# Attention with memory slots and two wide layers on one core: turns of a quarter, a quarter and a half for the first two batches

## The chip, the cores and the metric

The kernel runs on one core of a Trainium2 chip. The metric is the device time of one execution in microseconds (us), the median of the runs shown.

## The reference

Four batches of 576 tokens, 8 heads of 64. `phi` weighs the tokens of a head into 32 memory slots: a softmax over tokens, so its maximum and its sum run over 576 tokens. Queries attend to these 32 slots only. Two dense layers follow, 512 to 2048 to 512 each, with weights in float64.

```
a = exp(phi - max(phi, tokens)); a = a / (sum(a, tokens) + 1e-9)
k_m = einsum('bhsm,bhsd->bhmd', a, k); v_m = einsum('bhsm,bhsd->bhmd', a, v)
attn = softmax(q @ k_m^T / 8)                 # over the 32 slots
x = attn @ v_m                                # 2304 tokens x 512
x = leaky_relu(x @ w_in, 0.01) @ w_out        # first layer
out = mish(x @ w2_in) @ w2_out                # second layer
```

## The kernel before

A hand-written planner (class Order) puts all work in order before anything runs. Each piece of work (a task) has a priority in units of items, estimated engine durations, dependencies and buffers that it takes or uses. The planner walks through estimated time, at each moment gives a free engine the ready task of lowest priority, and so fixes the instruction order of every engine and of the DMA queue on SP. A task that takes a buffer may start at most WIN = 8 items ahead of the current item. On the chip each engine then runs its list strictly in order: an instruction whose input is late holds back all that stands behind it. For a load the planner assumes bytes divided by 300e3 per us, after those in front, plus fixed terms (L130, L294).

First layer. An item is one block of 128 hidden channels (m, 16 of them) for one half of a batch (sub, 288 tokens): 6 matmuls of at x vw into h_t (L862; vw is v_m times w_in for a quarter of four m, a chunk), two leaky relus on ACT, one giving hi_t, one e_t (L876), their difference lo_t on DVE (L883), and two items later 12 matmuls of w_out into four accumulators (L895). There are 128 items. At the end of a turn (a run of m for one batch) the accumulators are copied to x1, or added to it by DVE where an earlier turn wrote there (L940). Batches 0 and 1 share a chunk's decoded weights. Before, their turns are (L721): batch 0 chunk 0, batch 1 chunk 0, batch 0 chunk 1, batch 1 chunk 1, batch 0 chunks 2 and 3, batch 1 chunks 2 and 3, so that batch 1 starts at item 8; batches 2 and 3 follow whole, from items 64 and 96.

Preparation of a batch, in two groups g of four heads (kv_tasks, L429): load phi, k, v; the maximum over tokens by folding 6 rows to 3 (L449), then 3 to 1 by two further DVE operations (L451); a transpose on PE (L458), a reduce (L464), a diagonal matrix (L465), a broadcast by a matmul with ones (L471), four subtractions on DVE (L479), Exp on ACT; the same fold for the sum where b > 0, one matmul for the sum (L506); the matmuls for k_m and v_m (L495). score_tasks (L565) loads and transposes q (L582), multiplies, and half (L626) does the softmax over slots; the result is at_t, hi and lo (L298, L314). Group 1 of batches 0 and 1 has buffers of its own in a pool that is later closed (`sp = "s" if b < 2 and g == 1`, L430, L566); its space goes to the w_out blocks 8 to 15.

Weights: load_raw (L330) loads raw 512 KB of float64, decode (L352) makes float32 of it with ACT and DVE (L362, L364, L369, L371, L379, L389), hi_lo (L305) splits it in two parts. w_chunk(c) (L747) decodes four raw blocks of w_in into two win buffers and writes them to DRAM, from where later batches load them; wo_unit(m) (L733) does a block of w_out. Second-layer weights are decoded between the items from priority W2 = 48 on (L814) and written to DRAM. The second layer (units of L1208 and L1274) follows.

Priorities: batch 1's preparation starts A1 = 13 items ahead of its first item, group 1 S1 = 2 later; A2 = 30 and S2 = 10 for batches 2 and 3. Loads of w_out and w_in go WOL = 3 ahead of their decode, which is WO = 2 and WC = 4 ahead of the item. Buffers of a tag are given out in the order in which the code creates them (L795 to L810): chunk 0, batch 1 with its vw of chunk 0, chunk 1, and so on. FILL = 60 small matmuls (L776) occupy PE at the start.

Of the kernel before, what the change touches and what calls it, by code (L numbers as in the profile page):

```python
# [81 lines left out]
class Order:  # L82
# [10 lines left out]
    def run(self, window):  # L93
# [13 lines left out]
        while left:  # L107
            ready.sort(key=lambda t: (t.prio, t.n))
            hit = False
            for t in list(ready):  # L110
# [47 lines left out]
def kernel(  # L158
# [134 lines left out]
    def mb(shape_bytes):  # L293
        return shape_bytes / 300e3  # L294
# [134 lines left out]
    def kv_tasks(b, g, p0, dp):  # L429
        sp = "s" if b < 2 and g == 1 else ""  # L430
# [23 lines left out]
        t0 = keep(add({"DVE": 0.9}, p0, lambda e: fold(rmax, ALU.max), [l_phi], [rmax], [ph]))  # L454
        mt = ps_tag.new([P, PR])
        t1 = add(
            {"PE": 0.1}, p0 + dp,
            lambda e: nc.tensor.transpose(mt.make(), rmax.t[:, 0].rearrange("p h m -> p (h m)"), ident[:PR, :PR]),  # L458
            [t0], [mt], [rmax],
        )  # L460
        mx, dg = tags["mx" + sp].new([P, 1]), tags["dg" + sp].new([P, P])

        def fmax(e):
            nc.vector.tensor_reduce(out=mx.make(), in_=mt.t, axis=AX.X, op=ALU.max)  # L464
            nc.vector.tensor_scalar(out=dg.make(), in0=ident, scalar1=mx.t, scalar2=None, op0=ALU.mult)  # L465
# [916 lines left out]
```

## Time and profile before

| | |
|---|---|
| median of 3 runs | 804.36 us (802.5 to 805.64) |
| the profiled execution, its own time | 806.19 us |
| its span | 804.3 us |
| PE busy | 773.1 us, 96% |
| DVE, ACT busy | 558.4 us, 69%; 394.6 us, 49% |
| granted TensorE clock, mean | 0.982 |

The 20-us slices of the page show the stages: up to 42 us the preparation of batch 0, from 42 to 424 us the 128 items of the first layer with the preparation of batches 1 to 3 and the decoding of weights between them, from 424 us the second layer. A short matmul's record ends by a model, and a busy engine may still be at a low granted clock, so stretches are read with the clock beside them. Engines run their lists in order: an idle time in front of an instruction is put down to what it waited for, which need not be what PE needed.

### The profile page before, as it was taken

The numbers are of one execution on the slowest core, as the hardware profiler recorded it, in microseconds if no ns is written. First come the engines' busy times: TensorE is split into PE (matmuls) and PEld (weight loads), VectorE is DVE, ScalarE is ACT, GpSimd is POOL, SyncE is SP. The second block draws the span as 40 slices with busy tenths as digits, with TensorE's granted clock in tenths as the row PEclk, the third lists the DMA queues.
The fourth block names the chain that finished last, engine by engine and source line by source line (L and its number), as shares of the span: only waits on it lengthen the run. The fifth ranks groups of instructions, "written<-read, shape, count | busy, mean of one in ns | idle before, by whom it ended". The sixth has DMA issues, their size and how long they took to land.

```text
span 804.3 us, 13708 instructions
## 1 busy us (share of the span) xinstructions
PE 773.1 (96%) x5300; PEld 701.9 (87%) x5300; DVE 558.4 (69%) x1198; ACT 394.6 (49%) x857; POOL 0.7 (0%) x6
## 2 busy tenths in 40 slices
PE   7897999999999999999999999999999999999995
PEld 6686998898888998999999889888988998899884
DVE  4898879877876887661666667696666698566432
ACT  2667566745453555543555444454443355444322
POOL 0000000000000000000000000000000000000000
PEclk8899899999998999999999999999999999999998
DMA  9995599656867667400222210023010014000002
GB/s 219 257 275 162 174 266 274 216 168 223 268 218 220 207 199 261 160 27 1 79 79 78 81 53 26 27 80 106 26 51 29 1 53 131 27 27 27 0 1 78
DMA packets 43136, 97.61 MB, mean 121 GB/s; under 512 B 3904, under 2 KB 24384, under 8 KB 43072
## 3 DMA queue, kind: packets, MB, share of 16 engines
q1 hardware_dynamic: 42912, 96.48, 39.0%
q8 instruction: 41, 0.67, 0.3%
q10 hardware_dynamic: 160, 0.26, 0.1%
q14 instruction: 23, 0.19, 0.1%
HBM read 79.43 MB, written 17.30 MB: 120 GB/s over the span
## 4 chain that ended last, share of the span: by engine, by line
PE 73%; DMA 12%; DVE 9%; ACT 2%; issue 2%; SPq 1%; ACTq 0%; DVEq 0%
PE h_t L1208 22%; PE acc_t L1274 17%; PE acc_t L895 16%; PE misc_t L1274 8%; PE h_t L862 8%; DMA raw_t<-in_moe_w_out_dram 4%; DMA raws_t<-in_moe_w_in_dram 3%; DMA raw_t<-in_moe_w_in_dram 2%; DMA kv_t<-in_v_dram 2%; DMA kv_t<-in_k_dram 1%; DVE raw_t L389 1%; PE misc_t L699 1%; DVE lo_t L883 1%; PE misc_t L495 1%; DMA rawm_t<-in_moe_w_out_dram 1%
## 5 line engine op out<-in xcount | busy, mean ns | idle before, releaser
L895 PE MATMUL acc_t<-hi_t,wo_t 128*128 128x288 f32 x1024 | 163.6, 301 | 0.6 <-DVE x_t L300 0.3
L895 PEld LDWEIGHTS acc_t<-hi_t,wo_t 128*128 128x128 f32 x1024 | 144.6, 190 | 8.9 <-issue 4.5
L862 PE MATMUL h_t<-at_t,vw_t 128*128 128x288 f32 x768 | 127.0, 302 | 8.8 <-ACT e_t L876 5.5
L862 PEld LDWEIGHTS h_t<-at_t,vw_t 128*128 128x128 f32 x768 | 111.2, 192 | 11.6 <-ACT e_t L876 7.6
L876 ACT ACTIVATE hi_t<-h_t 128x288 fp32r<-128x288 f32 x128 | 52.9, 413 | 111.2 <-PE acc_t L895 96.9
L883 DVE TENSOR_TENSOR lo_t<-e_t,hi_t 128x288 fp32r<-128x288 f32 x128 | 58.7, 460 | 55.5 <-ACT e_t L876 26.2
L895 PE MATMUL acc_t<-lo_t,wo_t 128*128 128x288 f32 x512 | 91.6, 301 | 1.0 <-DVE lo_t L883 1.0
L1208 PE MATMUL h_t<-xt_t,vw_t 128*128 128x384 f32 x432 | 87.8, 338 | 0.0
L895 PEld LDWEIGHTS acc_t<-lo_t,wo_t 128*128 128x128 f32 x512 | 74.5, 188 | 10.9 <-issue 7.7
L1208 PE MATMUL h_t<-xt_t,wo_t 128*128 128x384 f32 x384 | 82.9, 337 | 0.0
L1208 PEld LDWEIGHTS h_t<-xt_t,vw_t 128*128 128x128 f32 x432 | 77.6, 188 | 6.0
L298 ACT ACTIVATE wo_t<-raw_t 128x512 fp32r<-128x512 f32 (+1 forms) x66 | 36.6, 561 | 86.6 <-PE h_t L1208 84.2
L1274 PE MATMUL acc_t<-wo_t,hi_t 128*128 128x512 f32 x288 | 78.2, 394 | 0.0
L1208 PEld LDWEIGHTS h_t<-xt_t,wo_t 128*128 128x128 f32 x384 | 69.1, 188 | 3.9
L1219 DVE TENSOR_TENSOR x_t<-x_t,h_t 128x384 f32<-128x384 f32 x96 | 52.7, 549 | 19.3 <-PE h_t L1208 19.2
L1274 PEld LDWEIGHTS acc_t<-wo_t,hi_t 128*128 128x128 f32 x288 | 53.6, 188 | 9.7
L298 ACT ACTIVATE vw_t<-raw_t 128x512 fp32r<-128x512 f32 x49 | 30.6, 631 | 58.6 <-PE h_t L1208 58.1
L876 ACT ACTIVATE e_t<-h_t 128x288 f32<-128x288 f32 x128 | 52.5, 410 | 0.1
L362 ACT ACTIVATE raw_t<-raw_t 128x512 f32<-128x512 f32 x43 | 33.2, 773 | 30.3 <-DMA raw_t<-in_moe_w_in_dram 16.9
L1274 PE MATMUL acc_t<-wo_t,lo_t 128*128 128x512 f32 x144 | 45.1, 392 | 0.0
L379 DVE TENSOR_SCALAR raw_t<-raw_t 128x512 uint16<-128x512 uint16 x50 | 37.7, 759 | 8.2 <-ACT raw_t L369 5.7
L1219 DVE TENSOR_TENSOR e_t<-e_t,h_t 128x384 f32<-128x384 f32 x24 | 13.3, 553 | 41.2 <-PE h_t L1208 41.1
(178 smaller groups left out, 1146.4 us busy)
## 6 DMA issues: line engine op xcount, KB each, us to landing
raw_t<-in_moe_w_out_dram SPq DMA_DIRECT2D x24, 512.0 KB, 5.3
win_t<-wscr SPq DMA_DIRECT2D x24, 512.0 KB, 5.2
raw_t<-w2scri SPq DMA_DIRECT2D x24, 512.0 KB, 3.2
raw_t<-in_moe_w_in_dram SPq DMA_DIRECT2D x22, 512.0 KB, 5.3
kv_t<-in_k_dram SPq DMA_DIRECT2D x8, 576.0 KB, 8.0
kv_t<-in_v_dram SPq DMA_DIRECT2D x8, 576.0 KB, 8.9
wscr<-win_t SPq DMA_DIRECT2D x8, 512.0 KB, 7.7
w2scri<-raw_t SPq DMA_DIRECT2D x8, 512.0 KB, 6.4
```

The lines of the kernel that those rows point to most:

```text
L298: nc.scalar.activation(out=o, in_=i, func=AF.Copy)
L362: nc.scalar.activation(out=hf(), in_=hf(), func=AF.Copy, scale=2.0 ** -112)
L379: lambda e: nc.vector.tensor_scalar(out=quarter(1), in0=quarter(3), scalar1=0x8000, scalar2=None, op0=ALU.bitwise_and),
L389: nc.vector.scalar_tensor_tensor(out=out, in0=hw(), scalar=3, in1=lw(), op0=ALU.logical_shift_left, op1=ALU.bitwise_or)
L495: nc.tensor.matmul(out=acc.t[M * h:M * (h + 1), :].rearrange("p (j d) -> p j d", j=2), lhsT=ph.t[:, h, r, :], rhs=kv.t[:, :, h, r, :], sta ...
L862: nc.tensor.matmul(out=h.t, lhsT=us[g][0].t[:, wi, j0:j0 + P], rhs=ats[g][0].t[:, ai, cols], start=(n == 0), stop=(n == 3 * NG - 1),)
L876: nc.scalar.activation(out=o, in_=h.t, func=AF.Prelu, alpha=0.01)
L883: lambda e: nc.vector.tensor_tensor(out=lb.make(), in0=eb.t, in1=hb.t.bitcast(F32), op=ALU.subtract),
L895: nc.tensor.matmul(out=ac[kk].t, lhsT=wu[0].t[:, wi, kk * P:(kk + 1) * P], rhs=(hb if src == 0 else lb).t, start=(first and (wi, src) == ( ...
L1208: nc.tensor.matmul(out=h.t, lhsT=w[:, wi, c0:c0 + P], rhs=xp[b, xi].ap()[:, j], start=(j == 0 and k3 == 0), stop=(j == 1 and k3 == 2),)
L1219: {"DVE": dve(NB2)}, prio, lambda e: nc.vector.tensor_tensor(out=out(), in0=in0(), in1=in1(), op=op), deps, take, use
L1274: nc.tensor.matmul(out=ac[t].t, lhsT=(lb if x else hb).t[:, t * P:(t + 1) * P], rhs=wu[0].t[:, wi, :], start=(first and (wi, x) == (0, 0)) ...
```

## The change

The turns of batches 0 and 1 become a list T: batch 0 chunk 0, batch 0 chunk 1, batch 1 chunks 0 and 1, batch 0 chunks 2 and 3, batch 1 chunks 2 and 3. Batch 1 starts at item 16, chunk 1 is needed at item 8. The code creates chunk and batch tasks in the same order. The folds stop at three rows: PE transposes all three, the reduce goes over 288 columns, three matmuls make the sum. The diagonal may go to ACT. For batch 0 (PB = 1) the subtraction is done by PE: phi times the identity and the diagonal, repeated by its access pattern, times minus one, into the same PSUM tile, in two halves, from which ACT takes Exp; for other batches the four subtractions become one of 768 elements. Only batch 0 has buffers of its own for group 1 (SB = 1). q0 is loaded ahead of kv0. The planner assumes 280e3 bytes per us, times 1.3 in duration for q, k and v, 1.5 for phi. Leads change: A1 10, S1 2.8, S2 2.6, V1 2.4, W2 56, W2S 2.9, WOL 1, WC 3.

```diff
-    LAG1=2, WIN=8, OB=2, RS=4, FILL=60, A1=13, S1=2,
-    A2=30, S2=10, V1=5, V2=14, W2=48.0, W2S=3.0, O='phi0 phi1 w0 kv0 q0 w1 kv1 w2 q1 w3', HF1=-8.0, HFS=1.0,
-    HFD=0.5, TOP=0.3, HI=0.2, WO=2.0, WOL=3.0, WC=4.0, WC0=-38.0, V0=3.0, COLD=20, GL=1.5, AL=5.0, XL=22.0,
+    LAG1=2, WIN=8, OB=2, RS=4, FILL=60, A1=10, S1=2.8,
+    A2=30, S2=2.6, V1=2.4, V2=14, W2=56.0, W2S=2.9, O='phi0 phi1 w0 q0 kv0 w1 kv1 w2 q1 w3', HF1=-8.0, HFS=1.0,
+    HFD=0.5, TOP=0.3, HI=0.2, WO=2.0, WOL=1, WC=3.0, WC0=-38.0, V0=3.0, COLD=20, GL=1.5, AL=5.0, XL=22.0, T='0:1 0:1 1:2 0:2 1:2', SB=1, PB=1,
+    DW=280e3, DQ=1.3, DP=1.5,
...
-        return shape_bytes / 300e3
+        return shape_bytes / K["DW"]
...
-        sp = "s" if b < 2 and g == 1 else ""
+        sp = "s" if b < K['SB'] and g == 1 else ""
...
-            t = buf.make()
             halves = [ph.t[:, :, r:r + R // 2].rearrange("p h r m -> p r h m") for r in (0, R // 2)]
-            nc.vector.tensor_tensor(out=t, in0=halves[0], in1=halves[1], op=op)
-            for r in (1, 2):
-                nc.vector.tensor_tensor(out=t[:, 0], in0=t[:, 0], in1=t[:, r], op=op)
+            nc.vector.tensor_tensor(out=buf.make(), in0=halves[0], in1=halves[1], op=op)
...
+            for r in range(R // 2):
+                nc.tensor.transpose(mt.t[:, r], rmax.t[:, r].rearrange("p h m -> p (h m)"), ident[:PR, :PR])
...
+            if e == "ACT":
+                nc.scalar.activation(out=dg.make(), in_=ident, func=AF.Copy, scale=mx.t)
+            else:
+                nc.vector.tensor_scalar(out=dg.make(), in0=ident, scalar1=mx.t, scalar2=None, op0=ALU.mult)
...
+        if b < K["PB"]:
...
+                    nc.tensor.matmul(out=o, lhsT=ident[:PR, :PR], rhs=ph.t[:, :, rs_], start=True, stop=False)
+                    mxs = dg.t.rearrange("p (h o m) -> p h o m", o=1, m=M).to_broadcast([P, HG, R // 2, M])
+                    nc.tensor.matmul(out=o, lhsT=minus, rhs=mxs, start=False, stop=True)
...
-            for h in range(HG):
-                nc.vector.tensor_tensor(
-                    out=ph.t[:, h], in0=ph.t[:, h], in1=bc.t[:, h].to_broadcast([PR, R, M]), op=ALU.subtract
-                )
...
+                lambda e: nc.vector.tensor_tensor(
+                    out=ph.t, in0=ph.t, in1=bc.t.to_broadcast([PR, HG, R, M]), op=ALU.subtract
+                ),
...
-    parts = [(0, NM // 4), (NM // 4, NM // 2), (NM // 2, NM)]
-    turns = [(b, *mm) for mm in parts for b in range(2)] + [(b, 0, NM) for b in range(2, B)]
+    chunk_turns, c_at = [], [0] * B
+    for x in K["T"].split() + [f"{b}:{NC}" for b in range(2, B)]:
+        b, n_c = map(int, x.split(":"))
+        chunk_turns.append((b, range(c_at[b], c_at[b] + n_c)))
+        c_at[b] += n_c
+    turns = [(b, 4 * cs[0], 4 * cs[-1] + 4) for b, cs in chunk_turns]
...
+    for b, cs in chunk_turns:
+        if b and not cs[0]:
+            next_batch(b)
         for c in cs:
+            if b:
+                next_vw(b, c)
+                continue
             w_chunk(c)
             for m in range(4 * c, 4 * c + 4):
                 wo_unit(m)
```

## Rows read from the trace of the kernel before

**Rows 1.** The page's line of engines: busy us, share of the span, instructions
```profile
PE 773.1 (96%) x5300; PEld 701.9 (87%) x5300; DVE 558.4 (69%) x1198; ACT 394.6 (49%) x857; POOL 0.7 (0%) x6
```

**Rows 2.** Stretches: busy us of PE, PEld, DVE, ACT, POOL; clock, DMA, GB/s
```profile
0.00:42.00 42.00, 33.60 (x394) 27.98 (x395) 27.04 (x76) 19.22 (x38) 0.70 (x6) 0.88 0.97 238
42.00:96.00 54.00, 48.00 (x436) 41.45 (x436) 48.65 (x124) 35.70 (x87) 0.00 (x0) 0.94 0.69 203
96.00:345.00 249.00, 241.85 (x2060) 221.22 (x2059) 195.13 (x433) 138.41 (x323) 0.00 (x0) 0.99 0.70 220
345.00:424.00 79.00, 79.00 (x583) 79.00 (x582) 42.60 (x88) 36.76 (x88) 0.00 (x0) 1.00 0.15 49
424.00:804.30 380.30, 370.70 (x1835) 332.30 (x1833) 245.00 (x482) 164.52 (x323) 0.00 (x0) 0.99 0.14 47
```

**Rows 3.** The same view, shorter stretches
```profile
80.00:90.00 10.00, 10.00 (x60) 9.64 (x68) 8.49 (x18) 4.58 (x12) 0.00 (x0) 0.71 0.42 159
240.00:260.00 20.00, 18.11 (x161) 16.29 (x160) 12.18 (x27) 7.74 (x19) 0.00 (x0) 0.83 0.70 205
300.00:320.00 20.00, 19.78 (x153) 18.40 (x154) 15.17 (x30) 11.82 (x28) 0.00 (x0) 1.00 0.81 268
```

**Rows 4.** Timeline of PE: start, us, engine, line, op; [idle before <- releaser]
```profile
41.84 1.83 PE L862 MATMUL h_t<-at_t,vw_t 128*128 128x288 f32 x12
...
49.63 1.52 PE L495 MATMUL misc_t<-kv_t,phi_t 96*32 96x128 f32 x48
...
77.76 1.02 PE L862 MATMUL h_t<-at_t,vw_t 128*128 128x288 f32 x4 [1.99 <-ACT at_t L298]
...
79.95 2.29 PE L862 MATMUL h_t<-at_t,vw_t 128*128 128x288 f32 x8 [1.17 <-DVE vw_t L314]
...
96.03 0.96 PE L862 MATMUL h_t<-at_t,vw_t 128*128 128x288 f32 x6
```

**Rows 5.** Timeline of DVE, before the first item and for batch 1
```profile
40.45 0.55 DVE L449 TENSOR_TENSOR rm_t<-phi_t 96x384 f32<-96x384 f32 x1
...
47.11 0.59 DVE L449 TENSOR_TENSOR rm_t<-phi_t 96x384 f32<-96x384 f32 x1
...
81.74 0.46 DVE L314 TENSOR_TENSOR at_t<-T_t,at_t 128x288 fp32r<-128x288 f32 x1
```

**Rows 6.** Timeline of SP's DMA issues, batch 1's entry
```profile
63.28 18.34 SPq L348 DMA_DIRECT2D raw_t<-in_moe_w_out_dram  x2
```

**Rows 7.** Waits of PE and ACT, 96 to 345 us: total us, times, longest
```profile
PE h_t L862 <- ACT e_t L876: 4.9, 5, 1.7
...
PE misc_t L582 <- DMA q_t<-in_q_dram: 1.4, 1, 1.4
...
ACT raw_t L362 <- DMA raw_t<-in_moe_w_out_dram: 11.5, 8, 2.8
...
ACT raw_t L362 <- DMA raw_t<-in_moe_w_in_dram: 6.2, 5, 3.0
```

**Rows 8.** One late load: SP's timeline, then ACT's
```profile
206.07 0.41 SPq L348 DMA_DIRECT2D raw_t<-in_moe_w_in_dram  x1
...
215.81 0.67 ACT L362 ACTIVATE raw_t<-raw_t 128x512 f32<-128x512 f32 x1 [2.96 <-DMA raw_t<-in_moe_w_in_dram]
```

**Rows 9.** Groups by line, DVE then PE: busy us, mean ns, idle
```profile
L451 DVE TENSOR_TENSOR rm_t<-rm_t 96x128 f32<-96x128 f32 x28 | 8.1, 288 | 1.0
...
L479 DVE TENSOR_TENSOR phi_t<-phi_t,misc_t 96x192 f32<-96x192 f32 x24 | 6.8, 345 | 1.3 <-PE misc_t L471 1.3
...
L940 DVE TENSOR_TENSOR x_t<-acc_t,x_t 128x288 f32<-128x288 f32 x32 | 12.4, 458 | 0.0
...
L582 PE MATMUL misc_t<-ident,q_t 96*128 96x96 f32 x60 | 8.3, 247 | 1.4 <-DMA q_t<-in_q_dram 1.4
...
L513 PE MATMUL misc_t<-ones,phi_t 96*32 96x1 f32 x96 | 1.4, 183 | 1.3 <-ACT phi_t L484 1.3
```

**Rows 10.** DMA issues until 85 us: queue, count, KB, median us to landing
```profile
kv_t<-in_k_dram SPq DMA_DIRECT2D x4, 576.0 KB, 10.8
```

More of the change, by code (lines that the diff above doesn't have):

```diff
@@ L435, in kv_tasks @@
         pl = p0 - 6
-        l_phi = load(pl if b else PPHI[g], ph.make, lambda: phi[b, hs].rearrange("h (p r) m -> p h r m", p=PR), 294912, (), [ph])
+        l_phi = load(pl if b else PPHI[g], ph.make, lambda: phi[b, hs].rearrange("h (p r) m -> p h r m", p=PR), 294912, (), [ph], (), K["DP"])
         def ld(e):
@@ L453, in kv_tasks @@
         rmax = tags["rm" + sp].new([PR, R // 2, HG, M])
[L454 to L459, printed above, removed]
-        )
[L461 to L465, printed above, removed]
@@ L483, in kv_tasks, with fmt @@
-        t4 = add({"DVE": 1.08}, p0 + 2 * dp, fsub, [t3], (), [ph, bc])
-        t5 = add({"ACT": act(768)}, p0 + 2.5 * dp, lambda e: nc.scalar.activation(out=ph.t, in_=ph.t, func=AF.Exp), [t4], (), [ph])
-        t6 = None
+        t0 = keep(add({"DVE": 0.58}, p0, lambda e: fold(rmax, ALU.max), [l_phi], [rmax], [ph]))
+        mt = ps_tag.new([P, R // 2, PR])
+        def fmt(e):
+            mt.make()
+            for r in range(R // 2):
+                nc.tensor.transpose(mt.t[:, r], rmax.t[:, r].rearrange("p h m -> p (h m)"), ident[:PR, :PR])
@@ new lines, in kv_tasks, with fdiff @@
+        t2 = add({"ACT": 0.21, "DVE": 0.21}, p0 + dp, fdg, [t2], [dg], [mx])
+        t6 = None
+        if b < K["PB"]:
+            t5 = []
+            for j, tag in enumerate((ps_tag, misc)):
+                df = tag.new([PR, HG, R // 2, M])
+                def fdiff(e, j=j, df=df):
+                    o = df.make().rearrange("p h r m -> p (h r m)")
+                    rs_ = slice(j * R // 2, (j + 1) * R // 2)
+                    nc.tensor.matmul(out=o, lhsT=ident[:PR, :PR], rhs=ph.t[:, :, rs_], start=True, stop=False)
+                    mxs = dg.t.rearrange("p (h o m) -> p h o m", o=1, m=M).to_broadcast([P, HG, R // 2, M])
+                    nc.tensor.matmul(out=o, lhsT=minus, rhs=mxs, start=False, stop=True)
+                t4 = add({"PE": 1.4}, p0 + 2 * dp + 0.01 * j, fdiff, [t2], [df], [dg, mx, ph])
+                t5.append(add(
+                    {"ACT": act(384, True)}, p0 + 2.5 * dp + 0.01 * j,
+                    lambda e, j=j, df=df: nc.scalar.activation(
+                        out=ph.t[:, :, j * R // 2:(j + 1) * R // 2], in_=df.t, func=AF.Exp
+                    ),
+                    [t4], (), [ph, df],
+                ))
+        else:
+            bc = ps_tag.new([PR, HG, 1, M])
+            t3 = add(
+                {"PE": 0.25}, p0 + 2 * dp,
+                lambda e: nc.tensor.matmul(
+                    out=bc.make().rearrange("p h o m -> p (h o m)"), lhsT=ones, rhs=dg.t, start=True, stop=True
+                ),
+                [t2], [bc], [dg, mx],
+            )
+            t4 = add(
+                {"DVE": 0.87}, p0 + 2 * dp,
+                lambda e: nc.vector.tensor_tensor(
+                    out=ph.t, in0=ph.t, in1=bc.t.to_broadcast([PR, HG, R, M]), op=ALU.subtract
+                ),
+                [t3], (), [ph, bc],
+            )
+            t5 = [add(
+                {"ACT": act(768)}, p0 + 2.5 * dp,
+                lambda e: nc.scalar.activation(out=ph.t, in_=ph.t, func=AF.Exp), [t4], (), [ph],
+            )]
@@ L505, in fsums @@
             if b:
-                nc.tensor.matmul(
-                    out=dn.t, lhsT=rs.t[:, 0].rearrange("p h m -> p (h m)"), rhs=ones[:PR, 0:1],
-                    start=True, stop=True,
-                )
+                for r in range(R // 2):
+                    nc.tensor.matmul(
+                        out=dn.t, lhsT=rs.t[:, r].rearrange("p h m -> p (h m)"), rhs=ones[:PR, 0:1],
+                        start=(r == 0), stop=(r == R // 2 - 1),
+                    )
                 return
```

55 lines of the change are left out of this document (21 added, 34 removed).

## The prediction, made before the changed kernel was run

> **What bounds the kernel now.** I read the page's line of engines first: PE is busy 773.1 us of a span of 804.3 [rows 1], so all that a change can win here is what PE waits, runs at a low clock, or no longer has to do. The busy time by stretch says where that is. From 424 us on the second layer runs, which the change doesn't touch, and from 345 to 424 us PE has no idle time [rows 2]. What is left: the time until the first item starts at 41.84 us [rows 4], batch 1's entry up to 96 us, and 96 to 345 us. From 42 to 96 us PE is busy 48.0 of 54 us and DVE 48.65, so both are near their limit; from 96 to 345 us PE is idle 7.2 of 249 us and DVE 54 us [rows 2]. The granted clock tells what a wait costs besides: 0.71 from 80 to 90 us is 2.9 us lost, 0.83 from 240 to 260 us is 3.4 us lost (ten and twenty us times what is missing to 1), both behind idle PE [rows 3].
>
> The timelines then say which wait ends last. Before item 8, the first of batch 1, PE sits idle until batch 1's at_t and vw_t are there (1.99 and 1.17 us, at 77.76 and 79.95 us) [rows 4], at the end of a preparation that took DVE from the fold at 47.11 us to the last part of at_t at 81.74 us [rows 5]. Meanwhile SP needs 18.34 us for two loads of w_out from 63.28 us on [rows 6]: they stand in order behind buffers that chunk 1's decode can't free, since batch 1 took the two win buffers first. From 96 to 345 us the waits of PE are short and of another kind: 4.9 us in five pieces for the leaky relu on ACT, 1.4 us for q [rows 7]. ACT isn't busy then; it waits in order for raw weights, 11.5 and 6.2 us [rows 7]. One case in full: a raw load issued at 206.07 us, with the 1.18 MB of k and v ahead of it, lets ACT begin at 215.81 us, after 2.96 us of waiting [rows 8].
>
> **The change part by part.** My sum is made against the profiled execution's 806.2 us (span 804.3 and 1.9 around it), which is 1.8 above the median of 804.36; that is taken off at the end.
>
> Start. Bytes ahead of the last block of chunk 0 stay the same; q0 only changes places with kv0. By 0.59 MB at the 238 GB/s of this stretch [rows 2] kv0 comes 2.5 us later, and the work of q0 fills that time; group 1's k and v are later still and set the end, so I count 0, at worst +1.5. Batch 0's subtractions and folds leave DVE, but early, while it has 15 of 42 us idle [rows 2]: nothing, and the four larger matmul pairs and transposes that replace them take the place of filler matmuls. Batch 1's first fold stands on DVE at 40.45 us [rows 5], just ahead of the first item: its two L451 operations go (2 x 0.29) [rows 9], and with the lead A1 shorter the remaining 0.55 us may stand behind. I take -1.0, between -2.5 (chunk 0 and at_t both earlier) and +1.5.
>
> Entry of batch 1. What PE has to do until item 16 is the same work before and after, in another order: 54 us from 42 to 96 us, of which 6.0 idle and 2.9 clock, so 45 us at the least. DVE's 48.65 us [rows 2] lose batch 1's shorter folds (8 x 0.29 = 2.3) and some 0.4 of its subtractions, and gain what becomes an add of chunk 1 onto batch 0 (8 operations of L940, 0.39 each by 12.4/32, of which ACT did more than half before as copies [rows 9]), about +1.6. So DVE needs 47.5 us, 6.5 below the 54 that the stretch takes. Chunk 1 is now wanted at item 8, and its chain (load, decode, vw) is shorter than batch 1's: its win buffers are free as soon as chunk 0's write to DRAM is done, and the 18.34 us on SP should go. Batch 1 gets eight more items, 19 us, before it is due. DVE has next to no slack in this, so I take not 6.5 but -4; the bounds are -6.5 and the first rival's +8.9.
>
> Waits from 96 to 345 us. The planner's new durations lengthen what it expects of a load. For the case of [rows 8], four earlier and later blocks aside: k, v and the raw block cost it 3.93 + 1.75 us before and 5.48 + 1.87 after, 1.7 us later, against 2.96 that ACT waited. A decode that is put later lets leaky relus pass ahead of it. PE's 6.3 us of waits [rows 7] and 3.4 of clock make 9.7; I take 40% of it, -4, since a longer guess removes part of each wait and none that it doesn't reach. The bounds are -9.7 and +2: the loads move from 3 to 1 item ahead of their decode (WOL), and group 1 of batches 2 and 3 comes 7.4 items earlier, so it meets the decoding of chunks 2 and 3, for which DVE is then needed as well; behind a late fold on DVE the lo_t of the next items are queued, and L895 waits for them. Moving the second layer's weights 8 items later (W2) goes to a stretch with DVE at 42.6 of 79 us and DMA at 0.15 [rows 2]; the cover is large: 0. One turn less takes 8 adds, 3.1 us, from DVE and nothing from PE: 0.
>
> The durations bring in a rule to weigh. The DMA is busy 0.97 of the time at 238 GB/s up to 42 us, where most bytes are rows of q, k, v and phi, and 0.81 at 268 GB/s from 300 to 320 us, where blocks of weights with long rows are moved [rows 2, 3]: 245 against 331 GB/s per busy time, a ratio of 1.35, near the new factor 1.3. The Trainium skill, DMA: Bandwidth & Descriptors, section Specifications, puts the smallest transfer for line rate at 512 B, and the rows of q, k, v (1536 B) and phi (768 B) are longer. By that rule the factors would be mere pessimism, the preparation of each batch would be planned 1.3 us late per load of k and v, and the sum would be some 1.3 us higher; the trace disagrees with it.
>
> More work for PE. Six groups of batches 1 to 3 get two more transposes, each at 8.3/60 = 0.14 us [rows 9], 1.7 us, and two more matmuls of one column, two records each, at 0.015 by L513 (1.4/96) [rows 9], 0.35. Where PE has no idle time this is paid: +2, between +0.3 and +3.6 (the isolated 183 ns of a record).
>
> Sum: 806.2 - 1.0 - 4 - 4 + 2 = 799.2; less 1.8 is 797.4 us.
>
> **The rivals.** First, slower: batch 1's group 1 comes late, because it has lost its own buffers. Its phi, k and v can be loaded only when group 0's matmuls for k_m have let go of the one buffer. Before, these stood at 49.63 us [rows 4], without any such wait for group 1. Now group 0's preparation stands behind chunk 1's decode on DVE, so 51 to 60 us; k and v then take 10.8 us to land [rows 10], 62 to 71; from the fold to the last at_t it took 34.6 us before [rows 5], so at_t is ready at 97 to 106 us against 96 in the trace for item 16 [rows 4]. At 102 PE waits 6 us longer than now and its clock falls again (2.9): 806.2 - 1.0 + 8.9 - 4 + 2 = 812.1, less 1.8 is 810.3. It decides from about 103 us without a fall of the clock. For it: the nearest path through DVE is the measured one, and q too has two buffers instead of eight. Against it: most of those 34.6 us were DVE's queue and a wait for loads, and DVE has less to do for batch 1 once chunk 1 is decoded.
>
> Second, no change: the entry's wait only moves from item 8 to item 16 (0 instead of -4), and half of the later waits' gain stays away, because a new order puts other loads late: 806.2 - 1.0 - 2 + 2 = 805.2, less 1.8 is 803.4. For it: DVE is at 90% from 42 to 96 us whatever the order. That the change doesn't do what it says: the planner puts the late decodes back in front of the relus, since DVE and ACT get the same list rule; that too ends at 803.
>
> **How the numbers follow.** A measurement of this kernel tells some 0.5%, 4 us, from no change. The forecast of 797.4 has 0.55; no change at 803.4 has 0.25; the slower rival at 810.3 has 0.2. Faster by over 0.5% is below 800.3: most of the forecast's cases and a few of the second rival's, 0.58. Within 0.5%, to 808.4: 0.25. Slower: 0.17. The range reaches down to 788, where the entry (-6.5), the start and most of the later waits are won (806.2 - 2.5 - 6.5 - 9.7 + 2 - 1.8 = 787.7), and up to 809, short of the slower rival's worst.
>
> **What would show it.** Right: the first item near 41 us; no issue of SP that spans 18 us; PE's wait ahead of batch 1 under 1 us and no slice below 0.9 in granted clock from 80 to 110 us; item 16 at 92 us or before; PE's waits for the leaky relu from 96 us on at 3 us or less; the second layer beginning at 417 us rather than 424. L451 is gone and L940 stands at 24. Wrong: an idle PE ahead of the first item of batch 1 with at_t as releaser, later than 96 us; waits of ACT for raw loads of 18 us or more in all; or a first item after 43 us. The second layer should keep its 380 us [rows 2]; if it moves, the cause lies outside these steps.

## The result, and the profile after

| | before | after |
|---|---|---|
| median us (range, runs) | 803.43 (799.59 to 805.64, 4) | 790.44 (789.74 to 791.38, 4) |
| profiled execution: us; span; granted clock | 806.19; 804.3; 0.982 | 791.02; 789.2; 0.993 |

The ratio is 0.9844, with a 95% interval of 0.9803 to 0.9885: 13.0 us less between the medians, 15.2 between the two profiled executions. That of before lies 2.8 us above its median, so some 2 us of the trace's difference belong to that execution and to no step.

The lines of after have moved: L862 is L894, L895 is L927, L876 is L908, L940 is L972, L348 is L351, L458 is L460, L506 is L540, L495 is L528, L1208 of the second layer is L1240. First the page's line of engines (busy us, share of the span, instructions), to set against [rows 1]:

```profile
PE 770.0 (98%) x5352; PEld 698.1 (88%) x5352; DVE 548.5 (69%) x1133; ACT 393.1 (50%) x863; POOL 0.7 (0%) x6
```

PE's busy time fell by 3.1 us and its span by 15.1: what went is idle time, 31.2 us before and 19.2 now, and low clock. The stretches of [rows 2] from 42 to 424 us, then the first two of [rows 3] (length, busy us of PE, PEld, DVE, ACT, POOL; granted clock, DMA share, GB/s):

```profile
42.00:96.00 54.00, 52.06 (x500) 46.41 (x499) 49.99 (x116) 36.93 (x90) 0.00 (x0) 1.00 0.62 200
96.00:345.00 249.00, 248.60 (x2164) 230.61 (x2163) 185.69 (x390) 138.99 (x333) 0.00 (x0) 1.00 0.71 218
345.00:424.00 79.00, 78.36 (x538) 76.56 (x537) 51.61 (x103) 40.72 (x93) 0.00 (x0) 1.00 0.20 69
...
80.00:90.00 10.00, 9.43 (x122) 8.23 (x121) 7.62 (x23) 5.93 (x16) 0.00 (x0) 1.00 0.24 84
240.00:260.00 20.00, 20.00 (x198) 18.67 (x198) 15.82 (x37) 12.29 (x32) 0.00 (x0) 1.00 0.88 262
```

From 42 to 96 us PE is busy 52.06 us where it was 48.00, and the clock is at 1.00 instead of 0.94. From 96 to 345 us it is idle 0.4 us instead of 7.2. Both stretches that stood at 0.71 and 0.83 of the full clock (2.4 GHz) are at 1.00. The second layer costs nearly what it did: from its first matmul to the end of the span 393.7 us before (410.56 to 804.3), 392.1 after (397.07 to 789.2).

PE's timeline at the start of the first item, at the last matmuls for group 1's k_m before it, and at item 16 (start, us, line; an idle time ahead would stand in brackets):

```profile
26.00 2.79 PE L528 MATMUL acc_t<-kv_t,phi_t 96*32 96x128 f32 x48
...
42.77 1.83 PE L894 MATMUL h_t<-at_t,vw_t 128*128 128x288 f32 x12
...
97.47 1.75 PE L894 MATMUL h_t<-at_t,vw_t 128*128 128x288 f32 x12
```

The first item starts at 42.77 us, 0.93 later than in [rows 4]. In front of item 16, the first of batch 1, PE has no idle time. SP's issues in the same stretch:

```profile
39.06 0.47 SPq L342 DMA_DIRECT2D raws_t<-in_moe_w_in_dram  x1
...
52.35 3.99 SPq L351 DMA_DIRECT2D raw_t<-in_moe_w_out_dram  x2
...
63.72 0.34 SPq L306 DMA_DIRECT2D phi_t<-in_phi_dram  x1
64.11 1.55 SPq L444 DMA_DIRECT2D kv_t<-in_k_dram  x1
```

The two loads of w_out that spanned 18.34 us [rows 6] take 3.99 now. Batch 1's group 1 gets its phi and k only at 63.72 and 64.11 us. The waits from 96 to 345 us, PE first, then ACT (total us, times, longest), against [rows 7]:

```profile
PE h_t L894 <- ACT e_t L908: 0.3, 1, 0.3
...
ACT raw_t L365 <- DMA raw_t<-in_moe_w_out_dram: 2.7, 4, 1.0
...
ACT raw_t L365 <- DMA raw_t<-in_moe_w_in_dram: 1.9, 3, 0.9
```

ACT's 11.5 and 6.2 us for raw weights are 2.7 and 1.9; PE's 4.9 for the relu is 0.3. What the shorter folds put on PE, and what a turn less takes from DVE (busy us, mean ns, idle), against [rows 9]:

```profile
L540 PE MATMUL misc_t<-ones,rm_t 96*128 96x1 f32 x36 | 4.4, 236 | 0.0
...
L460 PE MATMUL misc_t<-ident,rm_t 96*128 96x96 f32 x18 | 2.5, 245 | 0.0
...
L540 PEld LDWEIGHTS misc_t<-ones,rm_t 96*128 96x128 f32 x36 | 4.6, 191 | 0.0
...
L972 DVE TENSOR_TENSOR x_t<-acc_t,x_t 128x288 f32<-128x288 f32 x24 | 9.6, 447 | 1.9 <-PE acc_t L927 1.7
```

The matching groups on PE in before, for the sum and for the transposes:

```profile
L506 PE MATMUL misc_t<-ones,rm_t 96*128 96x1 f32 x12 | 1.8, 215 | 0.0
...
L458 PE MATMUL misc_t<-ident,rm_t 96*128 96x96 f32 x6 | 1.6, 260 | 0.1
```

Last, progress by items, which no single row gives: the start (us of the span) of the last of the twelve matmuls that add an item to acc_t, counted in each trace; the experiments' rows belong to the next section.

| item | 8th | 16th | 32nd | 64th | 96th | 128th |
|---|---|---|---|---|---|---|
| before | 75.5 | 106.6 | 151.7 | 247.3 | 343.6 | 425.4 |
| after | 68.2 | 97.3 | 143.1 | 238.1 | 328.2 | 409.7 |
| after, old durations | 74.4 | 98.8 | 146.2 | 243.0 | 335.9 | 422.1 |
| before, late durations | 73.0 | 103.3 | 143.6 | 238.2 | 328.9 | 410.2 |
| before, all durations | 73.0 | 114.4 | 154.7 | 249.3 | 339.0 | 420.3 |
| after, old turns | 68.2 | 118.9 | 160.0 | 255.1 | 346.5 | 428.3 |
| after, old turns, own buffers | 72.2 | 112.7 | 153.8 | 249.6 | 342.8 | 424.3 |
| after, own buffers for two | 68.5 | 109.7 | 150.8 | 246.3 | 336.2 | 418.1 |

After leads by 9.3 us at the 16th item, keeps that to the 64th, and gains 6 more by the 96th, past the place where before had its low clock (0.83 from 240 to 260 us [rows 3]).

### The profile page after: what moved, and what is told of

Its sections match the earlier page's. It is cut to its first block, busy times and chain, and to the rows that moved or that the text cites. A ratio compares the mean times of both kernels' runs of the same rounds, so it can differ in the third digit from the quotient of the medians.

```text
span 789.2 us, 13751 instructions
## 1 busy us (share of the span) xinstructions
PE 770.0 (98%) x5352; PEld 698.1 (88%) x5352; DVE 548.5 (69%) x1133; ACT 393.1 (50%) x863; POOL 0.7 (0%) x6
## 4 chain that ended last, share of the span: by engine, by line
PE 82%; DMA 3%; DVE 2%; ACT 1%; issue 1%; SPq 0%; DVEq 0%; ACTq 0%
PE h_t L1240 22%; PE acc_t L927 21%; PE acc_t L1306 17%; PE h_t L894 10%; PE misc_t L1306 8%; PE misc_t L733 2%; DMA raw_t<-in_moe_w_in_dram 2%; PE misc_t L528 1%; DMA raw_t<-in_moe_w_out_dram 1%; PE misc_t L616 0%; DVE raw_t L392 0%; PE misc_t L647 0%; DVE raw_t L382 0%; DVE lo_t L915 0%; PE misc_t L540 0%
## 5 line engine op out<-in xcount | busy, mean ns | idle before, releaser
L927 PE MATMUL acc_t<-hi_t,wo_t 128*128 128x288 f32 x1024 | 163.3, 299 | 1.4 <-ACT hi_t L908 0.7
L927 PEld LDWEIGHTS acc_t<-hi_t,wo_t 128*128 128x128 f32 x1024 | 142.8, 188 | 11.6 <-issue 6.2
L894 PE MATMUL h_t<-at_t,vw_t 128*128 128x288 f32 x768 | 123.6, 296 | 1.0 <-ACT e_t L908 1.0
L894 PEld LDWEIGHTS h_t<-at_t,vw_t 128*128 128x128 f32 x768 | 108.3, 188 | 3.1 <-ACT e_t L908 3.0
L908 ACT ACTIVATE hi_t<-h_t 128x288 fp32r<-128x288 f32 x128 | 52.6, 412 | 114.1 <-PE acc_t L927 104.0
L927 PE MATMUL acc_t<-lo_t,wo_t 128*128 128x288 f32 x512 | 90.6, 299 | 0.0
L1240 PE MATMUL h_t<-xt_t,vw_t 128*128 128x384 f32 x432 | 87.2, 336 | 0.0
L1240 PEld LDWEIGHTS h_t<-xt_t,vw_t 128*128 128x128 f32 x432 | 77.3, 188 | 6.1
L1240 PE MATMUL h_t<-xt_t,wo_t 128*128 128x384 f32 x384 | 82.6, 336 | 0.0
L927 PEld LDWEIGHTS acc_t<-lo_t,wo_t 128*128 128x128 f32 x512 | 74.7, 188 | 6.2 <-issue 5.2
L301 ACT ACTIVATE wo_t<-raw_t 128x256 fp32r<-128x256 f32 (+1 forms) x65 | 35.9, 559 | 88.7 <-PE h_t L1240 87.5
L1240 PEld LDWEIGHTS h_t<-xt_t,wo_t 128*128 128x128 f32 x384 | 68.8, 188 | 3.9
L301 ACT ACTIVATE vw_t<-raw_t 128x512 fp32r<-128x512 f32 x52 | 32.6, 631 | 57.8 <-PE h_t L1240 57.3
L908 ACT ACTIVATE e_t<-h_t 128x288 f32<-128x288 f32 x128 | 52.3, 410 | 0.0
L365 ACT ACTIVATE raw_t<-raw_t 128x512 f32<-128x512 f32 x45 | 32.9, 731 | 20.5 <-DMA raw_t<-in_moe_w_in_dram 15.8
```

What stands on the lines that cost most here:

```text
L301: nc.scalar.activation(out=o, in_=i, func=AF.Copy)
L365: nc.scalar.activation(out=hf(), in_=hf(), func=AF.Copy, scale=2.0 ** -112)
L894: nc.tensor.matmul(out=h.t, lhsT=us[g][0].t[:, wi, j0:j0 + P], rhs=ats[g][0].t[:, ai, cols], start=(n == 0), stop=(n == 3 * NG - 1),)
L908: nc.scalar.activation(out=o, in_=h.t, func=AF.Prelu, alpha=0.01)
L927: nc.tensor.matmul(out=ac[kk].t, lhsT=wu[0].t[:, wi, kk * P:(kk + 1) * P], rhs=(hb if src == 0 else lb).t, start=(first and (wi, src) == ( ...
L1240: nc.tensor.matmul(out=h.t, lhsT=w[:, wi, c0:c0 + P], rhs=xp[b, xi].ap()[:, j], start=(j == 0 and k3 == 0), stop=(j == 1 and k3 == 2),)
```

## The experiments

Each kernel ran beside the kernel before on the same chip (medians of before there: 801.56 to 802.57 us). The ratios are to those runs; after's is 0.9844. The theory that came out of the comparison: most of the gain is the planner's new durations, since a load that is expected later no longer has its decode put ahead of the leaky relus. The rivals: the new turns do it, by the entry of batch 1; or the shorter folds do it, by what they take from DVE.

### The durations

Experiment 1: after, with the old durations.

```diff
-    DW=280e3, DQ=1.3, DP=1.5,
+    DW=300e3, DQ=1.0, DP=1.0,
```

> The changed kernel with the planner's old transfer durations (300e3 bytes per us, no factors for q, k, v and phi). Theory A (the durations removed the late loads that ACT and DVE waited for in order, and with them the waits of PE): ACT's waits for raw loads between 90 and 345 us come back from 4.6 us towards 18 us, PE idles some 5 us more and its granted clock falls once, so 5 to 8 us slower than the changed kernel's 790.4, about 796 to 798. Rival B (turn order and shorter folds carry the gain, the durations only reshuffle): within 2 us of 790.4, and ACT's waits for raw loads stay below 8 us.

Measured: 802.61 us, ratio 1.001 (0.9989 to 1.0031). The whole gain is gone. Windows, then the waits of PE and ACT from 96 to 345 us:

```profile
42.00:96.00 54.00, 53.62 (x521) 48.62 (x521) 48.97 (x116) 34.48 (x83) 0.00 (x0) 1.00 0.55 165
96.00:345.00 249.00, 243.79 (x2107) 223.44 (x2106) 183.81 (x388) 136.92 (x321) 0.00 (x0) 1.00 0.70 215
345.00:424.00 79.00, 76.49 (x551) 75.40 (x550) 52.02 (x104) 40.33 (x92) 0.00 (x0) 1.00 0.27 87
...
PE h_t L894 <- ACT e_t L908: 3.0, 5, 1.0
...
ACT raw_t L365 <- DMA raw_t<-in_moe_w_in_dram: 14.2, 12, 3.9
ACT raw_t L365 <- DMA raw_t<-in_moe_w_out_dram: 9.7, 7, 2.5
```

The 8th item comes 6.2 us later than in after, but the entry of batch 1 is as good (53.62 us busy, clock 1.00; 16th item at 98.8 us), so the new turns work with the old durations too. Behind it ACT waits 23.9 us for raw weights instead of 4.6, and PE is idle 5.2 and 2.5 us in the two stretches where it was 0.4 and 0.6. The table of items shows the loss growing with every batch: 1.5 us at the 16th, 4.9 at the 64th, 12.4 at the 128th.

Experiment 2: before, with the new durations for loads of priority 16 and later alone (the loads for batches 0 and 1 and for chunks 0 and 1 keep the old ones). The factors for q, k, v and phi are in it too; their lines are left out here.

```diff
-    def mb(shape_bytes):
-        return shape_bytes / 300e3
+    def mb(shape_bytes, prio=0.0, slow=1.0):
+        return shape_bytes / 300e3 if prio < 16 else slow * shape_bytes / 280e3
...
-        return b, add({"SP": mb(P * 4096)}, prio, fn, (), [b])
+        return b, add({"SP": mb(P * 4096, prio)}, prio, fn, (), [b])
```

> The kernel before with the new durations only for loads of priority 16 and later (all of batches 2 and 3, chunks 2 and 3, the second layer's weights), so that the order around batch 1's entry stays exactly as before. Theory A (the durations gain 6 to 9 us after the entry, and in the run with the new durations everywhere the entry lost that again): the entry keeps its 6 us of idle PE, ACT's waits for raw loads after 96 us fall from 17.7 us to under 8, 793 to 798 in all. Rival B: 800 to 804.

Measured: 792.18 us, ratio 0.9876 (0.9839 to 0.9913).

```profile
42.00:96.00 54.00, 48.92 (x457) 41.02 (x456) 49.79 (x124) 36.89 (x90) 0.00 (x0) 0.97 0.67 206
96.00:345.00 249.00, 247.75 (x2140) 230.65 (x2139) 198.74 (x440) 141.29 (x331) 0.00 (x0) 1.00 0.69 218
...
PE h_t L862 <- ACT at_t L298: 2.0, 1, 2.0
PE h_t L862 <- DVE vw_t L314: 1.2, 1, 1.2
...
ACT raw_t L362 <- DMA raw_t<-in_moe_w_in_dram: 5.0, 5, 1.9
...
ACT raw_t L362 <- DMA raw_t<-in_moe_w_out_dram: 1.7, 3, 1.0
```

This is before with nothing but other guesses: the waits ahead of item 8 are still there (2.0 and 1.2 us, as in [rows 4]), but ACT's waits for raw weights are 6.7 us instead of 17.7, and PE's idle time from 96 to 345 us is 1.3 instead of 7.2. Some 10 us (802.57 to 792.18 between the medians) come from the durations alone, and at the 128th item this kernel stands at 410.2 us, after at 409.7.

The two traces also say how far two executions differ. PE's instructions here are those of before, in the same order, up to the 916th, and those of DVE and ACT are the same up to about 102 us. Yet the next one of PE starts at 103.4 us in this trace and at 107.0 in that of before. These 3.6 us belong to the execution or its chip and not to the durations. Of the 14.2 us between the two spans (804.3 and 790.1) some 10.6 are left, which agrees with the medians.

Experiment 3: before, with the new durations for every load.

```diff
-        return shape_bytes / 300e3
+        return shape_bytes / K["DW"]
...
-        l_kv = add({"SP": mb(1179648)}, pl + 0.2 if b else PKV[g], ld, (), [kv])
+        l_kv = add({"SP": K["DQ"] * mb(1179648)}, pl + 0.2 if b else PKV[g], ld, (), [kv])
```

> The kernel before with only the new transfer durations. Theory A: ACT's waits for raw loads from 96 to 345 us fall from 17.7 us to under 8, the wait of PE for the leaky relu from 4.9 us to under 2, the low clock from 240 to 260 us goes; 5 to 8 us faster, about 796 to 798. Rival B: within 2 us of 803.4, with as much waiting in other places.

Measured: 802.91 us, ratio 1.0021 (1.0000 to 1.0041). Windows, then PE's longest wait from 42 to 96 us (line numbers are one higher than in before):

```profile
42.00:96.00 54.00, 42.26 (x365) 35.95 (x365) 46.87 (x121) 32.35 (x77) 0.00 (x0) 0.82 0.63 185
96.00:345.00 249.00, 248.77 (x2160) 229.65 (x2160) 195.66 (x433) 141.01 (x331) 0.00 (x0) 1.00 0.70 220
...
PE h_t L863 <- ACT vw_t L299: 4.0, 1, 4.0
```

The waits went as the theory has it, the time as the rival has it. From 96 to 345 us PE is idle 0.2 us, less than in after. But with the old turns the entry breaks: idle 11.7 of 54 us at a clock of 0.82, and the 16th item at 114.4 us instead of 106.6. That gives the later gain back. The parts don't add up: the durations need either the old guesses for the first loads or another entry of batch 1, which experiments 7 to 9 look into.

Experiment 4: after with DW=300e3, but the factors for q, k, v and phi left in; and experiment 5, the converse, DW=280e3 with factors of 1.

```diff
-    DW=280e3, DQ=1.3, DP=1.5,
+    DW=300e3, DQ=1.3, DP=1.5,
```

> The changed kernel with 300e3 bytes per us for all loads but the factors 1.3 and 1.5 for q, k, v and phi kept. If the short rows of q, k, v and phi are what the old durations got wrong: within 3 us of 790.4. If the general rate is: towards the 802.6 of the run with all old durations, 797 or more, with ACT's waits for raw loads above 12 us after 90 us.

```diff
-    DW=280e3, DQ=1.3, DP=1.5,
+    DW=280e3, DQ=1.0, DP=1.0,
```

> The changed kernel with the rate of 280e3 bytes per us but no factors for q, k, v and phi. Theory from the rows (short rows move at three quarters of the rate, so the factors are needed): ACT's waits for raw loads after 96 us rise from 5 us to 10 or more, 795 to 800. The line-rate rule (rows of 768 and 1536 B move like long ones, the factors are pessimism): 787 to 792, no more waits than before.

Measured: experiment 4 798.02 us, ratio 0.9950 (0.9921 to 0.9978); experiment 5 794.24 us, ratio 0.9899 (0.9867 to 0.9930). PE's stretch and ACT's waits for raw weights from 96 to 345 us of experiment 4, then the waits of 5:

```profile
96.00:345.00 249.00, 241.90 (x2099) 222.28 (x2098) 182.74 (x385) 136.58 (x322) 0.00 (x0) 1.00 0.70 210
...
ACT raw_t L365 <- DMA raw_t<-in_moe_w_in_dram: 12.7, 8, 3.6
ACT raw_t L365 <- DMA raw_t<-in_moe_w_out_dram: 8.6, 6, 3.7
```

```profile
ACT raw_t L365 <- DMA raw_t<-in_moe_w_out_dram: 6.9, 7, 3.2
ACT raw_t L365 <- DMA raw_t<-in_moe_w_in_dram: 5.9, 9, 1.6
```

Without the slower rate 21.3 us, without the factors 12.8, with both 4.6, with neither 23.9 (all at L365; L372 waits 2.0 more in experiment 5, 0.4 at most in the others): each of the two takes waits away, the rate more. In experiment 4 PE is idle 7.1 us in this stretch, where after has 0.4. In time the rate is worth 8 us (0.9950 against 0.9844). What the factors are worth is left open by experiment 6.

Experiment 6: how much one order of the planner differs from a neighbour: after with DW=279e3, 0.4% from 280e3.

```diff
-    DW=280e3, DQ=1.3, DP=1.5,
+    DW=279e3, DQ=1.3, DP=1.5,
```

> The changed kernel with the planner's rate at 279e3 instead of 280e3 bytes per us, a change of 0.4% of a duration that has no meaning of its own but puts the instructions of all engines in a partly different order. Theory A (the gain follows from the amount by which loads are expected later, so a neighbouring order is as good): within 4 us of 790.4. Rival D (the changed kernel's order is one lucky case, and any other order of the same parameters falls back by around 10 us, as the old durations did): 796 us or more.

Measured: 794.55 us, ratio 0.9895 (0.9864 to 0.9926). PE's longest wait in it from 96 to 345 us:

```profile
PE misc_t L580 <- DVE vw_t L317: 2.6, 1, 2.6
```

It isn't in after: another order, another collision. ACT's waits for raw weights are 4.1 and 1.1 us, 5.2 in all, near after's 4.6: by this measure the two orders are neighbours, by their time they differ. So a change of the durations that means nothing moves the time by 4 us (0.9895 against 0.9844), and no difference of that size between two orders is put down to a cause here. The 3.8 us of experiment 5 are such a difference.

### The turns and the buffers

Experiment 7: after, with the old turns and the leads A1, S1 and V1 that belong to them.

```diff
-A1=10, S1=2.8, ... V1=2.4, ... T='0:1 0:1 1:2 0:2 1:2'
+A1=13, S1=2, ... V1=5, ... T='0:1 1:1 0:1 1:1 0:2 1:2'
```

> The changed kernel with the old turns (batch 1's chunk 0 from item 8) and batch 1's old leads (A1 13, S1 2, V1 5), the rest as changed. Theory A (the entry gained because batch 1 is due eight items later): the wait ahead of batch 1's first item returns, 3 us of idle PE and a fall of the clock, and the items 16 to 32 start 5 to 8 us later; about 796 to 799. Rival C (the entry gained through the shorter folds on DVE and the buffer order, not the turns): 790 to 793.

Measured: 810.33 us, ratio 1.0104 (1.0073 to 1.0135). Window and PE's longest waits from 42 to 96 us:

```profile
42.00:96.00 54.00, 42.69 (x371) 32.98 (x370) 43.90 (x105) 29.43 (x70) 0.00 (x0) 0.83 0.74 203
...
PE misc_t L540 <- DVE rm_t L451: 2.6, 1, 2.6
PE h_t L894 <- ACT at_t L301: 2.2, 1, 2.2
```

Experiment 8: the same, and batch 1's group 1 has its own buffers again, as in before.

```diff
-A1=10, S1=2.8, ... V1=2.4, ... T='0:1 0:1 1:2 0:2 1:2', SB=1
+A1=13, S1=2, ... V1=5, ... T='0:1 1:1 0:1 1:1 0:2 1:2', SB=2
```

> The changed kernel with the old turns, batch 1's old leads and SB = 2, so that only durations, folds and the other leads are new. The run with old turns and one set of buffers stood at 810.3, its entry 21 us worse; this one tells how much of that was the missing buffers. If the buffers did it (old turns need batch 1 early, one set makes it late): 795 to 800, idle and low clock together from 42 to 96 us like before the change, some 9 us. If the turns did it alone: 805 or more.

Measured: 805.55 us, ratio 1.0038 (1.0022 to 1.0054). PE's waits from 42 to 96 us:

```profile
PE h_t L894 <- ACT vw_t L301: 8.5, 1, 8.5
PE h_t L894 <- DVE vw_t L317: 3.1, 1, 3.1
```

With new durations and old turns PE is idle 11 to 12 us in the entry, at a clock of 0.83 to 0.87, and the 16th item comes 15 to 22 us later than in after. Experiment 7 is 19.9 us slower than after and slower than either of its expectations. Own buffers take back 4.8 of these, little more than the 4 us of experiment 6.

Experiment 9: after, new turns, with own buffers for batch 1's group 1. If the first rival is right that the missing buffers hold this group back, this gains.

```diff
-SB=1
+SB=2
```

> The changed kernel with SB = 2: batch 1's group 1 keeps its own phi, k, v and q buffers, as before the change. Theory of the slower rival of the prediction (the lost buffers hold group 1 back): its phi, k and v are issued some 15 us earlier than at 63.7 us, batch 1 is ready earlier and the kernel gains 2 to 4 us, 786 to 789. Against it: item 16 waits for DVE and PE, not for these loads; 790 to 794, since the pool of these buffers is closed later and the w_out blocks 8 to 15 come later.

Measured: 799.42 us, ratio 0.9960 (0.9942 to 0.9979): it loses 9 us, against both of its expectations. SP's issues, then the windows:

```profile
40.88 0.40 SPq L306 DMA_DIRECT2D phi_t<-in_phi_dram  x1
41.33 0.52 SPq L444 DMA_DIRECT2D kv_t<-in_k_dram  x1
...
43.28 5.57 SPq L306 DMA_DIRECT2D qs_t<-in_q_dram  x4
51.78 0.35 SPq L351 DMA_DIRECT2D raw_t<-in_moe_w_in_dram  x1
...
55.14 0.47 SPq L342 DMA_DIRECT2D raws_t<-in_moe_w_in_dram  x1
...
70.00:80.00 10.00, 6.92 (x73) 3.61 (x73) 9.90 (x24) 7.49 (x18) 0.00 (x0) 0.55 0.27 108
...
42.00:96.00 54.00, 48.73 (x449) 42.41 (x448) 47.18 (x106) 35.44 (x85) 0.00 (x0) 0.87 0.64 190
```

With buffers free, batch 1's group 1 loads at 40.88 to 43.28 us: its phi, k, v and q stand in the queue ahead of chunk 1's w_in (51.78 and 55.14 us; in after the first of these raws_t was issued at 39.06), which is wanted first. The 8th item is done at 68.5 us, as in after, but the next L894 starts only at 82.05, where after had it at 68.4; from 70 to 80 us PE runs at 0.55 of the full clock. The lack of buffers that the rival feared is what keeps these loads back until their turn in after.

Turns and buffers don't add up either. The new turns with their leads are worth 19.9 us with one set of buffers (810.33 to 790.44) and 6.1 with own ones (805.55 to 799.42); own buffers gain 4.8 us with the old turns and cost 9.0 with the new.

### The folds

Experiment 10: after with before's folds, subtractions and sums.

```diff
-            nc.vector.tensor_tensor(out=buf.make(), in0=halves[0], in1=halves[1], op=op)
+            nc.vector.tensor_tensor(out=t, in0=halves[0], in1=halves[1], op=op)
+            for r in (1, 2):
+                nc.vector.tensor_tensor(out=t[:, 0], in0=t[:, 0], in1=t[:, r], op=op)
...
+            for h in range(HG):
+                nc.vector.tensor_tensor(
+                    out=ph.t[:, h], in0=ph.t[:, h], in1=bc.t[:, h].to_broadcast([PR, R, M]), op=ALU.subtract
+                )
```

> The changed kernel with the old folds, four subtractions and one matmul for the sum (batch 0's subtraction on DVE too), turns, leads and durations as changed. Theory A (the shorter folds mostly move work off DVE where DVE isn't the last, and cost PE 3.5 us of transposes and sums in batches 1 to 3): within 3 us of 790.4, PE busy some 3 us less, DVE busy some 12 us more. Rival C (DVE's relief carries the entry of batch 1): 4 us or more slower, 795 to 799, with PE waiting for DVE between 42 and 100 us.

Experiment 11: after with long folds, one transpose and one sum for batches 1 to 3; batch 0 as in after.

```diff
+        n_r = 1 if b else R // 2
...
-            for r in range(R // 2):
+            for r in range(n_r):
...
-            t6 = add({"DVE": 0.58}, p0 + 3 * dp, lambda e: fold(rs, ALU.add), t5, [rs], [ph])
+            t6 = add({"DVE": 0.9}, p0 + 3 * dp, lambda e: fold3(rs, ALU.add), t5, [rs], [ph])
```

> The changed kernel with long folds, one transpose and one matmul for the sum in batches 1 to 3, while batch 0 keeps the short fold and the subtraction on PE. Theory E (what the old folds gained in the earlier run, 787.8, is the 3.5 us of PE work in batches 1 to 3, in a stretch where PE has no idle time): 786.5 to 788.5. Rival F (it came from batch 0, whose first item started 5 us earlier with the old folds): 790 to 792.

Experiment 12: after with batch 0's subtraction back on DVE, folds short.

```diff
-PB=1
+PB=0
```

> The changed kernel with PB = 0: batch 0's subtraction goes back to DVE (one operation of 768 elements and a broadcast matmul), the short folds stay everywhere. Theory E (the start gains little, since DVE and the loads set batch 1's entry anyway): 789 to 792 although the first item may start up to 5 us earlier. Rival F: 786.5 to 788.5 with a first item near 38 us and item 16 some 2 us earlier.

Measured: 787.76 us, ratio 0.9815 (0.9779 to 0.9851); 789.32, 0.9830 (0.9804 to 0.9857); 789.89, 0.9847 (0.9824 to 0.9871). All three intervals hold after's 0.9844. Experiment 11 lies between its two expectations and decides for neither. The line of engines of experiment 10:

```profile
PE 762.1 (97%) x5300; PEld 692.0 (88%) x5300; DVE 561.2 (71%) x1194; ACT 390.4 (50%) x854; POOL 0.7 (0%) x6
```

PE's busy time is 7.9 us less than in after, DVE's 12.7 more, and the time is the same within what can be told. So the shorter maxima and sums, taken as one part of the change, bring nothing measurable: they move work from DVE to PE, and PE is the bound. That they cost something isn't shown either: experiment 10's runs (784.37 to 789.13 us) all lie below after's (789.74 to 791.38), but the 2.7 us between the medians are less than the 4 of experiment 6.

Experiment 12 also says what the start is worth. Its first matmuls of L894:

```profile
37.56 0.40 PE L894 MATMUL h_t<-at_t,vw_t 128*128 128x288 f32 x1
...
39.00 0.53 PE L894 MATMUL h_t<-at_t,vw_t 128*128 128x288 f32 x2 [1.05 <-DVE vw_t L317]
...
40.27 2.49 PE L894 MATMUL h_t<-at_t,vw_t 128*128 128x288 f32 x9 [0.73 <-DVE at_t L303]
```

It begins 5.2 us earlier than after, but in pieces, with waits for vw_t and at_t; at the 16th item it leads by 1.7 us and at the 128th by 0.2.

## Why the prediction was right and where it was wrong

The sign and the range held (797.4 forecast, 788 to 809; 790.44 measured). The places did too: both gains lie where the sum put them. The size was half of what came: 7.0 us were forecast, 13.0 measured between the medians.

Start, forecast -1.0, bounds -2.5 and +1.5: measured +0.9, with the wrong sign. Against experiment 2's trace, which starts the first item at 40.35 us in before's order, it is +2.4, outside the bounds. L451's two additional operations are gone from the place before the first item, as said. But batch 0's subtraction is now PE's, and the step that failed is that this work only "takes the place of filler matmuls": with the subtraction back on DVE (experiment 12) the first item starts 5.2 us earlier. By which chain isn't shown; the 48 matmuls for group 1's k_m, at least, took 2.79 us from 26.00 us on, against 1.71 in before. Experiment 12 also shows why the error was cheap: the earlier start reaches the end with nothing.

Entry of batch 1, forecast -4, bounds -6.5 and +8.9: by the two profiled executions -7.3 from 42 to 96 us, past the bound. Idle time and lost clock were 6.0 and 3.2 us (54 times 0.06); they are 1.9 and 0. By finished items it is 9.3 at the 16th. But experiment 2's trace, with the same order in this stretch, loses only 5.1 and 1.6 us there, and against it the entry gained 4.8. So the mechanism came as put, and that -4 was the wrong size isn't shown. The reason given for it, "DVE has next to no slack", is what failed: DVE is busy 49.99 us instead of the 47.5 of the working, more than before's 48.65, and PE waits nowhere for it. The busy share of DVE was no measure of lateness: in experiments 7 to 9, which only change turns, leads and buffers, DVE is busy 43.90 to 47.71 us in this stretch and the 16th item comes 12 to 22 us later than in after. The mark that I had set for it, item 16 at 92 us, was the wrong one: 97.47 is later than before's 96.03, because in before L862 of that item ran some 10 us ahead of the finished items (16th at 106.6), and in after it doesn't run ahead (16th at 97.3).

Waits from 96 to 345 us, forecast -4, bounds -9.7 and +2: measured -6.8 of idle time and -3.4 of clock, together -10.2, past the bound. This is the term that was mis-sized most. The mechanism is as it was put: the decode of a block that is expected later is queued behind relus, ACT waits 4.6 us instead of 17.7, PE's wait for e_t falls from 4.9 to 0.3. The step that failed is "40% of it, since a longer guess removes part of each wait": it took almost all. Experiment 2 shows it alone (ratio 0.9876), experiment 1 its absence (1.001). With the idle PE the low clock from 240 to 260 us [rows 3] went too.

More work for PE, forecast +2, bounds +0.3 and +3.6: measured +3.5. L540 takes 4.4 us in 36 records where L506 took 1.8 in 12, and L460's misc_t form 2.5 us where L458 took 1.6. The 0.015 us that I took for a one-column matmul from L513 was wrong here by eight times; a record of L540 costs 0.12. The measured sum is just inside the bound of 3.6, but that bound doesn't follow from its row: 24 records at 183 ns are 4.4 us, with the transposes 6.1. L513 loads 32 columns for a record, L540 128, and those loads take 0.13 us each (4.6/36 on PEld), as long as the record itself.

Sum of the measured terms: 0.9 - 7.3 - 10.2 + 3.5 = -13.1, against -15.2 in the profiled executions; 2.1 us have no term. The second layer is 1.6 of these. The terms are those of two single executions, and before's lies above its median; the 3.6 us of experiment 2 say how much of them can be that.

The rivals. The first (batch 1's group 1 late) named a chain that came as described: its phi and k were issued at 63.72 us, later than the 51 to 60 of the working, and its last at_t part was done at 99.2 us, inside the 97 to 106. But it decides from 103, and PE didn't wait. Experiment 9 turned its premise around: own buffers cost 9 us. The second (the wait moves to item 16) is refuted by the row at 97.47 us, with no idle time ahead of it. Its first half would have been true with the new durations and the old turns (experiments 3, 7 and 8), where the entry ate the later gain. The third (the change doesn't do what it says) fell with ACT's waits.

What the additive sum hid is the interaction. New turns without new durations: 1.001. New durations for late loads without new turns: 0.9876. New durations for all loads without new turns: 1.0021 on before's folds and buffers, 1.0038 on after's folds, 1.0104 with one set of buffers besides. All together: 0.9844. The prediction gave each part its own term and priced entry and waits alike; by the runs, the durations carry the gain, and the new turns with one set of buffers are what lets the first loads be planned with them. What turns, leads and buffers bring beyond experiment 2 (1.7 us by the medians, 2.6 by the ratios) is below what one order differs from its neighbour. The leads of the loads and of batches 2 and 3 (WOL, WC, W2, S2) were never changed by themselves; what they do stays open.

The rule that was weighed (the Trainium skill, DMA: Bandwidth & Descriptors, section Specifications: line rate from 512 B on) would make the factors for q, k, v and phi needless. The trace of before disagrees: counted packet by packet from 96 to 345 us, bytes over the time that the packets took, a DMA engine moved rows of 4096 B at 21.3 bytes per ns, rows of 1536 B (q, k, v) at 16.4 and rows of 768 B (phi) at 18.1, ratios of 1.30 and 1.18 to the factors' 1.3 and 1.5. That the length of the row is the cause isn't shown, since q, k, v and phi also go to 96 partitions and the weights to 128. Experiment 5 leaves the factors out and ACT's waits for raw weights rise from 4.6 to 12.8 us, as they would if loads behind those land later than planned. In time, 3.8 us against a spread of 4, it stays undecided.

As for the marks: no SP issue spans 18 us (10.27 is the longest from 30 to 345 us); no slice from 80 to 110 us is below 0.9; PE waits 0.3 us for relus, 3 were allowed; L451's small operations are gone and L972 stands at 24; the first item, at 42.77 us, missed 41; the second layer begins 13.5 us earlier, where 7 was written.

## What to carry to other kernels

Where a planner writes fixed orders for in-order queues, plan each load with the landing time that the trace shows under load, and rather later: guesses shorter by 7% for weights and by 28% for q, k and v (280/300, and that by 1/1.3) put ACT to waiting for weights while finished matmuls waited for their relu, and cost some 10 us of 803. Try parts of a change together as well as alone: here turns and durations each decide whether the other one gains or loses, and a buffer more can lose 9 us by letting a load out of turn. Run a neighbour of the chosen setting first, to know below which difference (4 us here) one order says nothing about its cause.

## What the runs showed of the hardware

Idle time of PE cost more than its length in some places, since a low granted clock went with it. In experiment 9 PE was idle 3.1 us from 70 to 80 us at a clock of 0.55, near the lower level (1.2 GHz), and 48 matmuls for k_m took 2.79 us there, against 1.52 in [rows 4]. In before 6.0 us idle from 42 to 96 us went with 3.2 us of clock, in experiment 3 11.7 us idle with 9.7 (54 times 0.18). It isn't so everywhere: from 96 to 345 us PE was idle 7.1 us in experiment 4, 2.3 of them in one wait, and 5.2 in experiment 1, and the clock of that stretch was 1.00 in both.

A matmul of one column took 0.12 us a record (4.4/36) where 128 columns are loaded for each (L540), and 0.015 (1.4/96) where 32 are (L513 [rows 9]). That the load makes the difference isn't shown.

Two executions of one order were 3.6 us apart after some 105 us (experiment 2 and before).
